# Splitting the last output tile, and two changes to a hand-written instruction plan, in a fused attention and feed-forward kernel

## The chip, the core and the metric

The kernel runs on one core of a Trainium2 chip. The metric is device time in microseconds for one execution, lower being better; the time quoted for a kernel is the median of several executions. The core has a matrix engine (TensorE, "PE" in the profile, with its weight loads listed as "PEld"), a vector engine (DVE), a scalar engine (ACT), a general engine (POOL) and a queue engine (SP) that here does nothing but issue transfers. Each engine runs its own instructions strictly in the order in which the program lists them, and waits on semaphores for the others.

## The reference

Two stages follow each other. The first is a block-wise linear attention with decay over 4 batches of 8 heads, 768 positions and 64 channels; the second a feed-forward layer on the 3072 tokens that result.

```python
for b in range(nb):                                   # blocks of 64 positions
    intra = einsum('bhic,bhjc->bhij', qb, kb) * Dmask
    intra = einsum('bhij,bhjd->bhid', intra, vb)
    inter = einsum('bhid,bhde->bhie', qb * lam_pow, kv_state)
    out[:, :, sl] = intra + inter
    kv_state = lam_block * kv_state + einsum('bhsd,bhse->bhde', kb * rev_pow, vb)
...
h = x @ w_in                                          # [3072, 512] @ [512, 2048]
g = where(h >= 1, h, where(h <= -1, 0, (h + 1) ** 2 / 4))
return g @ w_out                                      # [3072, 2048] @ [2048, 512]
```

## The kernel before

**Tiles.** The kernel works on 24 chunks of 128 positions (six to a batch) and on 6 stages of 512 tokens (four chunks each). For each chunk c it loads k and v (`ld`, 256 KB each) and for each pair of chunks q (`lq`, 512 KB), multiplies q and k by powers of lambda while casting to bfloat16 (`cast`, `cq`), transposes both, computes masked scores and the chunk's output, and updates a running state with keys and values. A stage then multiplies its 512 tokens by `w_in` (16 steps `l1`), applies the activation (ACT `r`, then three DVE steps `g`), and multiplies by `w_out` (16 steps `l2`: four tiles of 128 tokens, each in four steps `kg` of four matmuls). Each finished tile of 128 x 512 results is copied from PSUM to SBUF by ACT (`y`, line 398) and stored by SP (`st`, line 402).

**Names and lines.** The steps that the text follows are: `t` (transpose of keys; on PE for chunks 0 to 5, line 263, and as a transfer on the SP queue from chunk 6 on, line 284, tile kT); `qT` (transpose of queries; as transfers on SP from pair 3 on, line 287); `kb` and `kT` (copies of transposed keys from PSUM by DVE, lines 273 and 280); `u` (state update on PE, line 293) and `ub` (its cast by ACT, line 297); `s` (scores on PE, line 304 for chunks 0 to 3 and 312 after) and `m` (mask, DVE, lines 320 and 322); `o` (chunk output on PE, lines 329 and 332) and `x` (its copy by ACT into the tokens of the stage, line 339); `la` (the first four `l1` steps of stage 0 on three of its four chunks, line 353); `l1` (line 360); `l2` (line 393). Loads of k and v stand on line 439 (x1f and x2f in the profile), of q on line 435 (x0f), the casts of k on line 240 and of q on line 244 (tiles ks and qs), those of v on line 258 (vi).

**The order of the work** is written by a planner in the kernel itself, `run_plan`. Each step is entered with `add(key, engine, ns, function, needs, due, ...)`: an assumed duration, the steps that it needs, and for some a due time. The planner walks through an assumed time, gives each engine as its next step the ready one with the earliest due time, and in the end emits all instructions in that order. The times only decide the order: on the chip each engine follows the order and waits for what is really late. A step that becomes ready earlier in the plan is placed earlier in its engine's list.

A transfer's arrival is assumed from a single stream with a rate per step (`dma`). For loads of k and v from chunk 8 on, and of q from pair 4 on, 5000 ns are added:

```python
if x.key[0] in ("ld", "lq") and x.key[1] >= (FAR if x.key[0] == "ld" else FAR // 2):
    x.end += SLACK
```

On SP a transposing transfer has due -2 and a load a due time of 0 or a little more, so that a transpose that is ready goes ahead of a load; a load becomes ready when the buffer of the chunk six earlier (k, v) or the pair three earlier (q) has been cast. Before SP may issue a transfer, the plan asks that the third one back has been moved (`RING = 3`). A transpose counts as ready 2000 ns after its cast on POOL (`XSL`). Due times of the steps `l1` and `l2` lie 1057 ns apart from 22000 on in the order of `l_seq`, where they alternate between one stage's `l2` and the next one's `l1`; those of the steps of a chunk are counted back from the first `l1` that needs it (`o_due`), for scores another 2500.

**PSUM.** There are eight banks: two for `ph`, two for `py`, one each for `pt`, `pu`, `ps` and `po`. Outputs of `l2` use `py`, those of `l1` `ph`. The transposes `t` of chunks 0 to 5 use `pt`, which is also the second score bank of chunk 3 and of the chunks after it.

Of the kernel before, what the change touches and what calls it, by code (L numbers as in the profile page):

```python
# [23 lines left out]
def kernel(  # L24
# [31 lines left out]
    LD = 6  # L56
    LQ, NQ2 = 3, 3
    NO = 8
    XQ = 3
    RW, NR = 2, 3  # L60
    XT, NQT, NQK, RING = 6, 4, 4, 3
# [99 lines left out]

    LAT, FILL = 70, 170
    FAR, SLACK, XSL = 8, 5000, 2000
    ops, OPS = [], {}

    class Op:
# [9 lines left out]
    def run_plan(free):  # L176

        users = {x.key: [] for x in ops}
        for x in ops:
            x.needs = [OPS[y] for y in x.keys if y in OPS]  # L180
            for y in x.needs:
                users[y.key].append(x)
        left = {x.key: len(x.needs) for x in ops}
        topo = [x for x in ops if not x.needs]
        for x in topo:
            for u in users[x.key]:
                left[u.key] -= 1
                if left[u.key] == 0:
                    topo.append(u)
        assert len(topo) == len(ops)  # L190
        for x in reversed(topo):
            d = [u.due - u.ns - x.extra - LAT for u in users[x.key] if not u.dma]
            x.due = min(d + ([x.own] if x.own is not None else []), default=1e9)
            if x.dma or x.key[0] in ("l1", "l2"):
                x.due = x.own
        left = {x.key: len(x.needs) for x in ops}
        ready = {e: [] for e in free}
        for x in topo:
            if not x.needs:
                ready[x.eng].append((0, x))  # L200
        out_seq, xfer, dma_free = [], [0] * RING, 0
        while len(out_seq) < len(ops):
            t, e = min((max(free[e], min(r for r, _ in lst), xfer[-RING] if e == "SP" else 0), e)
                       for e, lst in ready.items() if lst)
            r, x = min(((r, x) for r, x in ready[e] if r <= t), key=lambda p: (p[1].due, p[0]))
            ready[e].remove((r, x))
            ns = x.ns + (720 if x.perf and free["POOL"] > t else 0)
            free[e] = t + ns
            x.t, x.end = t, t + ns + x.extra
            if x.dma:  # L210
                dma_free = max(dma_free, t + (1300 if e == "SP" else 2100)) + x.dma
                x.end = dma_free + 1400
                if x.key[0] in ("ld", "lq") and x.key[1] >= (FAR if x.key[0] == "ld" else FAR // 2):
                    x.end += SLACK
                if e == "SP":
                    xfer.append(dma_free)
            out_seq.append((t, len(out_seq), x))
            for u in users[x.key]:
                left[u.key] -= 1
                if left[u.key] == 0:  # L220
                    ready[u.eng].append((max(y.t if y.eng == u.eng and y.key != u.gate else y.end + (XSL if u.eng == "SP" and y.eng == "POOL" and u.dma == 640 else LAT) for y in u.needs), u))
        for t, _, x in sorted(out_seq, key=lambda p: p[:2]):
            if DBG:
                print(f"{t / 1e3:9.3f} {x.due / 1e3:9.3f} {x.eng:5s} {x.ns:6.0f} {x.key}")
            x.fn()
# [161 lines left out]
                op=AX.mult)  # L387

    def f_l2(s, ms, kg):
        if kg == 0:  # L390
            py_t[s, ms] = pp_y.tile([128, d_model], F32, name="py", tag="py")
        for ko in range(4 * kg, 4 * kg + 4):
            nc.tensor.matmul(py_t[s, ms], lhsT=gT[s][:, ko, ms * 128:(ms + 1) * 128], rhs=w_out_sb[:, ko, :],  # L393
                             start=(ko == 0), stop=(ko == FO - 1))

    def f_y(s, ms):
        osb[s, ms] = op.tile([128, d_model], F32, name="osb", tag="osb")
        nc.scalar.copy(out=osb[s, ms], in_=py_t[s, ms])  # L398

    def f_st(s, ms):  # L400
        m0 = s * MS + ms * 128
# [78 lines left out]
    for c in range(NCH):  # L480
        od, cb = o_due(c), c % NCB
        lastu = c - 1 if cb else c - 2
        m = c // 2
        e = "DVE" if c < CPS else "POOL"
        add(("cast", c, 1), e, 690 if e == "DVE" else 1060, lambda c=c, eng=(nc.vector if e == "DVE" else nc.gpsimd): cast(c, eng),
            [("ld", c, 1), ("cast", c - 1, 1), ("t", c - NQK), ("u", c - NQK)])
        add(("cast", c, 2), "ACT", 640, lambda c=c: cast_v(c),
            [("ld", c, 2), ("o", c - NV), ("u", c - NV), ("cast", c - 1, 2)])
        for i in range(2 if c % 2 == 0 else 0):
            old = ("tq", m - NQK // 2, i)  # L490
            add(("cq", m, i), "POOL", 1060, lambda m=m, i=i: cast_q(m, i, nc.gpsimd),
                [("lq", m), ("cq", m, 0) if i else None, old, ("qT",) + old[1:]])
            if m < XQ:
                add(("tq", m, i), "PE", mm(*[128] * 4), lambda m=m, i=i: f_tq(m, i),
                    [("cq", m, i)] + ([("kT", c - 1), ("m", c - 1, 1), ("tq", m, 0) if i else None] if c >= CPS else []),
                    due=od - 6000, extra=FILL)
                add(("qT", m, i), "ACT", 600, lambda m=m, i=i: f_qT(m, i), [("tq", m, i)])
            else:
                add(("qT", m, i), "SP", 1200, lambda m=m, i=i: f_qx(m, i), [("cq", m, i), ("o", 2 * (m - NQ2) + 1)], due=-2, dma=640)
        if c < XT:  # L500
            add(("t", c), "PE", mm(*[128] * 4), lambda c=c: f_t(c),
                [("cast", c, 1), ("kT", c - 1), ("kb", c - 1, 0), ("kb", c - 1, 1), ("m", c - 1, 1) if c > 2 else None,
                 ("qT", m, 0) if c >= CPS and c % 2 == 0 and m < XQ else None, ("qT", m, 1) if c >= CPS and c % 2 == 0 and m < XQ else None],
                due=od - 6000, extra=FILL)
        else:
            add(("t", c), "SP", 1200, lambda c=c: f_kx(c), [("cast", c, 1), ("m", c - NQT, 1)], due=-2, dma=640)
        if CPS <= c < XT:
            add(("kT", c), "DVE", 450, lambda c=c: f_kT(c), [("t", c), ("m", c - NQT, 1)])
        for hi in range(2 if c < CPS else 0):
            add(("kb", c, hi), "DVE", 365, lambda c=c, hi=hi: f_kb(c, hi), [("t", c), ("s", c - NKB, 1)])  # L510
        if cb < NCB - 1:
            add(("u", c), "PE", mm(*[128] * 4), lambda c=c: f_u(c),
                [("cast", c, 1), ("cast", c, 2), ("ub", lastu, 0), ("ub", lastu, 1), ("u", lastu)], due=od - 4000, extra=FILL)
            for hi in range(2):
                add(("ub", c, hi), "ACT", 372, lambda c=c, hi=hi: f_ub(c, hi), [("u", c), ("o", c - NUB + 1)])
        if c >= CPS:
            add(("s", c, 0), "PE", mm(*[128] * 4) + 190, lambda c=c: f_s2(c),
                [("kT", c) if c < XT else ("t", c), ("qT", m, 0), ("qT", m, 1), ("m", c - 1, 0), ("m", c - 1, 1)], due=od - 2500, extra=FILL)
        for h in range(2):
            if c < CPS:  # L520
                add(("s", c, h), "PE", mm(*[128] * 4), lambda c=c, h=h: f_s(c, h),
                    [("kb", c, 0), ("kb", c, 1), ("qT", m, 0), ("qT", m, 1), ("m", c - 1, 0) if not h else ("t", c)], due=od - 3000 + 100 * h, extra=FILL)
            add(("m", c, h), "DVE", 690, lambda c=c, h=h: f_m(c, h), [("s", c, h if c < CPS else 0), ("o", c - 3), ("m", c, 0) if h else None])
        add(("o", c), "PE", mm(*[128] * (12 if cb else 8)), lambda c=c: f_o(c),
            [("m", c, 1), ("cast", c, 2), ("ub", c - 1, 0) if cb else None, ("ub", c - 1, 1) if cb else None,
             ("x", c - 1), ("o", c - 1)], due=od, extra=FILL)
        add(("x", c), "ACT", 600, lambda c=c: f_x(c), [("o", c), ("x", c - 1), ("l1", (c // CPS - 2) * FO - 1)])
# [27 lines left out]
    for n2, (_, s, ms, kg) in enumerate(l2_order):  # L555
# [3 lines left out]
        else:  # L559
            need = [("g", (s * FO + 4 * kg + 3) // RW)]  # L560
        y = s * CPS + ms
        add(("l2", n2), "PE", mm(*[512] * 4), lambda a=(s, ms, kg): f_l2(*a),
            need + [("w", 1, kg), ("l2", n2 - 1), ("y", y - 2) if kg == 0 else None], due=l_due[2, s, ms, kg], extra=FILL)
        if kg == 3:
            add(("y", y), "ACT", 600, lambda a=(s, ms): f_y(*a), [("l2", n2), ("y", y - 1), ("st", y - NO)])
            add(("st", y), "SP", 550, lambda a=(s, ms): f_st(*a), [("y", y), ("st", y - 1)], due=0.055, dma=780)

# [31 lines left out]
```

## Time and profile before

| what | value |
|---|---|
| time, median of 4 runs | 226.08 us (225.9, 226.05, 226.1, 229.04) |
| time of the profiled execution | 227.34 us |
| its span, first to last instruction | 225.5 us |
| PE, busy | 206.8 us, 92% |
| DVE, busy | 141.0 us, 63% |
| ACT, busy | 123.9 us, 55% |
| POOL, busy | 62.3 us, 28% |
| moved by transfers | 34.40 MB, 153 GB/s over the span |
| granted clock of PE, mean | 0.996 |

The page gives for each engine the busy time, its share of the span and the number of instructions. The row of digits for an engine cuts the span into 40 equal slices and gives the busy share of each in tenths. Times in the views count from the first instruction. In the timeline a line reads: start, duration, engine, line of the code, operation, what is written and read, the number of instructions merged, and in brackets the idle time ahead of it with what ended it. The duration of a merged line runs from the first start to the last end. "SPq" is the time that the SP queue took to issue a transfer, not the transfer itself; the DMA view gives the time from the start of the issue to the landing.

### The profile page before, as it was taken

How to read it: one execution, taken by the hardware profiler on the slowest of the kernel's cores; microseconds unless marked ns; L12 is line 12 of the kernel's file. 1: busy time of each engine (PE TensorE's matmuls, PEld its weight loads, DVE VectorE, ACT ScalarE, POOL GpSimd, SP SyncE). 2: the span in 40 equal slices, each digit the busy share in tenths (PEclk: the TensorE clock that was granted, in tenths of full speed). 3: DMA queues.
4: the chain of work that ended last, by engine and by line, in shares of the span. 5: the costliest groups of instructions: out<-in, count | busy, mean ns of one | idle time of the engine just before them, and what ended most of it. 6: DMA issues, size and time to landing. Idle time of an engine off the chain costs nothing.

```text
span 225.5 us, 4659 instructions
## 1 busy us (share of the span) xinstructions
PE 206.8 (92%) x1888; PEld 135.4 (60%) x1888; DVE 141.0 (63%) x216; ACT 123.9 (55%) x222; POOL 62.3 (28%) x65
## 2 busy tenths in 40 slices
PE   0597996999997989999999999999999999999992
PEld 0486533677576777777766766777767644444440
DVE  4577395889958855697555668577565564464200
ACT  3556767547448466557637556676645544554121
POOL 7380084217616150746131027430000000000000
PEclk9999999999999999999999999999999999999998
DMA  5999999999797899999999799979201101111121
GB/s 134 242 189 201 196 239 186 179 214 221 123 257 124 215 160 204 133 245 134 241 149 324 217 260 229 208 168 158 41 33 49 47 0 49 47 47 46 47 96 48
DMA packets 89830, 34.40 MB, mean 153 GB/s; under 512 B 70352, under 2 KB 86736, under 8 KB 89808
## 3 DMA queue, kind: packets, MB, share of 16 engines
q1 hardware_dynamic: 85440, 29.89, 64.1%
q0 software_dynamic: 4224, 4.19, 11.6%
q8 instruction: 15, 0.25, 0.5%
q14 instruction: 7, 0.06, 0.1%
q10 hardware_dynamic: 144, 0.00, 0.0%
HBM read 27.27 MB, written 6.29 MB: 149 GB/s over the span
## 4 chain that ended last, share of the span: by engine, by line
PE 73%; DMA 17%; SPq 4%; POOL 2%; ACT 1%; issue 1%; POOLq 0%
PE py L393 35%; PE ph L360 29%; DMA x1f<-in_k_dram 5%; DMA w_in_sb<-in_moe_w_in_dram 4%; DMA x2f<-in_v_dram 4%; PE po L332 3%; PE ps L312 3%; SPq L439 3%; DMA x0f<-in_q_dram 2%; DMA kT<-ks 2%; PE po L329 1%; POOL qs L244 1%; PE pu L293 1%; SPq L435 1%; POOL w_in_sb L154 1%
## 5 line engine op out<-in xcount | busy, mean ns | idle before, releaser
L368 ACT ACTIVATE r<-ph,one 128x512 bf16<-128x512 f32 (+2 forms) x96 | 64.8, 679 | 56.9 <-PE ph L360 39.1
L393 PE MATMUL py<-w_out_sb,gT 128*128 128x512 bf16 x384 | 95.4, 379 | 0.0
L360 PE MATMUL ph<-xT,w_in_sb 128*128 128x128 bf16 (+2 forms) x880 | 94.0, 255 | 0.2 <-ACT r L368 0.2
L360 PEld LDWEIGHTS <-w_in_sb 128*128 128x128 bf16 x880 | 65.3, 98 | 23.5 <-issue 1.0
L393 PEld LDWEIGHTS <-gT 128*128 128x128 bf16 x384 | 35.5, 98 | 33.5 <-DVE gT L384 0.2
L376 DVE TENSOR_SCALAR t<-r 128x1024 bf16<-128x1024 bf16 x48 | 26.5, 551 | 40.8 <-ACT r L368 40.8
L379 DVE TENSOR_TENSOR w<-r,t 128x1024 bf16<-128x1024 bf16 x48 | 38.9, 810 | 1.5
L384 DVE TENSOR_TENSOR gT<-w,t 128x1024 bf16<-128x1024 bf16 x48 | 38.5, 801 | 1.6
L240 POOL TENSOR_TENSOR ks<-x1f,tab_k 128x512 bf16<-128x512 f32 x20 | 25.2, 1260 | 46.9 <-DMA x1f<-in_k_dram 19.5
L244 POOL TENSOR_TENSOR qs<-x0f,tab_q 128x512 bf16<-128x512 f32 x24 | 27.1, 1149 | 29.8 <-DMA x0f<-in_q_dram 20.6
L398 ACT COPY osb<-py 128x512 f32<-128x512 f32 x24 | 14.1, 586 | 16.3 <-PE py L393 12.8
L322 DVE TENSOR_TENSOR sc<-ps,causal 128x512 bf16<-128x512 f32 x20 | 13.8, 688 | 13.8 <-PE pt L312 13.8
L339 ACT CAST xT<-po 128x512 bf16<-128x512 f32 x24 | 14.1, 588 | 8.9 <-PE po L332 5.9
L332 PE MATMUL po<-sc,vi 128*128 128x128 bf16 x192 | 18.9, 224 | 0.0
L258 ACT CAST vi<-x2f 128x512 bf16<-128x512 f32 x24 | 14.8, 618 | 5.9 <-DMA x2f<-in_v_dram 5.8
L297 ACT CAST ubd<-pu 64x256 bf16<-64x256 f32 x40 | 14.6, 365 | 5.1 <-PE pu L293 4.7
L332 PEld LDWEIGHTS <-vi 128*128 128x128 bf16 x192 | 14.9, 101 | 2.3 <-issue 0.4
L329 PE MATMUL po<-qT,ubd 128*128 128x128 bf16 x80 | 14.7, 221 | 0.2 <-ACT xT L339 0.2
L322 DVE TENSOR_TENSOR sc<-pt,causal 128x512 bf16<-128x512 f32 x20 | 13.6, 680 | 0.0
L293 PE MATMUL pu<-vi,ks 128*128 128x128 bf16 x80 | 8.2, 228 | 2.2 <-ACT vi L258 2.1
L312 PE MATMUL ps<-qT,kT 64*128 64x128 bf16 x80 | 7.9, 219 | 2.1 <-DMA kT<-ks 2.1
L263 PE MATMUL pt<-ident,ks 128*128 128x128 bf16 x24 | 2.8, 248 | 7.2 <-DVE ks L240 7.0
(50 smaller groups left out, 81.0 us busy)
## 6 DMA issues: line engine op xcount, KB each, us to landing
x1f<-in_k_dram SPq DMA_DIRECT2D x24, 256.0 KB, 4.9
x0f<-in_q_dram SPq DMA_DIRECT2D x12, 512.0 KB, 5.7
x2f<-in_v_dram SPq DMA_DIRECT2D x24, 256.0 KB, 4.8
out_dram<-osb SPq DMA_DIRECT2D x24, 256.0 KB, 2.4
w_in_sb<-in_moe_w_in_dram POOLq DMA_DIRECT2D x4, 512.0 KB, 9.0
w_out_sb<-in_moe_w_out_dram POOLq DMA_DIRECT2D x4, 512.0 KB, 8.7
qT<-qs SPq DMA_TRANSPOSE x18, 4.0
kT<-ks SPq DMA_TRANSPOSE x18, 3.6
```

Of the source, the lines that this page charges most:

```text
L240: eng.tensor_tensor(ks[c], qkv_ld[c, 1], _bc(tab_k[:, c % NCB, :], 2, D), op=AX.mult)
L244: eng.tensor_tensor(qs[m, e], qkv_ld[m, 0][:, :, e], _bc(tab_q[:, e, m % (NCB // 2), :], 2, D), op=AX.mult)
L258: nc.scalar.copy(out=v_out(vi[c % NV]), in_=qkv_ld[c, 2].rearrange("p (a b) d -> p a b d", b=2))
L322: nc.vector.tensor_tensor(sc_sb[c][:, g], pst[c, g], _bc(causal, 1, HP), op=AX.mult)
L329: nc.tensor.matmul(po[:, hp], lhsT=ubd[(c - 1) % NUB][:, hp, :], rhs=q_cols(c, hp), start=True, stop=False)
L332: nc.tensor.matmul(po[:, hp], lhsT=vi[c % NV][:, hp, hi].rearrange("p a d -> p (a d)"), rhs=sc_sb[c][:, hi, hp, :], start=(cb == 0 and hi ...
L360: nc.tensor.matmul(ph[:, j * m:(j + 1) * m], lhsT=w_in_sb[:, ko, (ni + j) * 128:(ni + j + 1) * 128], rhs=xT[s][:, ko, part * m:(part + 1) ...
L368: nc.scalar.activation(out=r_t[grp][:, i, cs], in_=ph_t[s, ni, part][:, cs], func=AF.Relu, bias=one[:, 0:1])
L376: nc.vector.tensor_scalar(t_t[grp], r, 0.5, 1.0, op0=AX.mult, op1=AX.min)
L379: nc.vector.tensor_tensor(w_t[grp], r, t_t[grp], op=AX.subtract)
L384: nc.vector.tensor_tensor(gT[s][:, f - RW * n:f, part * m:(part + 1) * m], w_t[grp].rearrange("p a (b m) -> p (a b) m", m=m), t_t[grp].rea ...
L393: nc.tensor.matmul(py_t[s, ms], lhsT=gT[s][:, ko, ms * 128:(ms + 1) * 128], rhs=w_out_sb[:, ko, :], start=(ko == 0), stop=(ko == FO - 1))
```

## The change

The change has three parts. The last output tile, of stage 5 and tokens 384 to 511 of it, is computed in two column parts of 384 and 128 columns: the first runs through all 16 blocks of the inner dimension in a bank of `py`, then the second in a bank of `ph`. Each part is copied by DVE, where ACT copied the tile, and stored by a transfer of its own. Second, the 5000 ns that the planner adds to arrivals become 2500 for k and v of chunks 8 and 9 and q of pair 4. Third, the transpose `t` of chunk 3 no longer needs the mask `m` of chunk 2 (the condition begins at chunk 4).

```diff
+    LAST, CUT = (NST - 1, CPS - 1), 384
...
+    NEAR = 2500
...
                 if x.key[0] in ("ld", "lq") and x.key[1] >= (FAR if x.key[0] == "ld" else FAR // 2):
-                    x.end += SLACK
+                    x.end += SLACK if (x.key[1] if x.key[0] == "ld" else 2 * x.key[1]) >= 10 else NEAR
...
     def f_l2(s, ms, kg):
+        if (s, ms) == LAST:
+            i = kg // 2
+            if kg % 2 == 0:
+                pl, nm = ((pp_y, "py"), (pp_h, "ph"))[i]
+                py_t[s, ms, i] = pl.tile([128, d_model], F32, name=nm, tag=nm)
+            cs = (slice(0, CUT), slice(CUT, d_model))[i]
+            for ko in range(FO // 2 * (kg % 2), FO // 2 * (kg % 2 + 1)):
+                nc.tensor.matmul(py_t[s, ms, i][:, cs], lhsT=gT[s][:, ko, ms * 128:(ms + 1) * 128],
+                                 rhs=w_out_sb[:, ko, cs], start=(ko == 0), stop=(ko == FO - 1))
+            return
...
+    def f_y2(i):
+        s, ms = LAST
+        cs = (slice(0, CUT), slice(CUT, d_model))[i]
+        if i == 0:
+            osb[s, ms] = op.tile([128, d_model], F32, name="osb", tag="osb")
+        (nc.vector.tensor_copy, nc.vector.tensor_copy)[i](osb[s, ms][:, cs], py_t[s, ms, i][:, cs])
+
+    def f_st2(i):
+        s, ms = LAST
+        m0 = s * MS + ms * 128
+        cs = (slice(0, CUT), slice(CUT, d_model))[i]
+        nc.sync.dma_start(out=out[m0:m0 + 128, cs], in_=osb[s, ms][:, cs])
...
-                [("cast", c, 1), ("kT", c - 1), ("kb", c - 1, 0), ("kb", c - 1, 1), ("m", c - 1, 1) if c > 2 else None,
+                [("cast", c, 1), ("kT", c - 1), ("kb", c - 1, 0), ("kb", c - 1, 1), ("m", c - 1, 1) if c > 3 else None,
...
-        add(("l2", n2), "PE", mm(*[512] * 4), lambda a=(s, ms, kg): f_l2(*a),
+        add(("l2", n2), "PE", mm(*[512] * 4) if (s, ms) != LAST else mm(*[CUT if kg < 2 else d_model - CUT] * 8), lambda a=(s, ms, kg): f_l2(*a),
...
-        if kg == 3:
+        if (s, ms) == LAST:
+            if kg % 2:
+                i = kg // 2
+                add(("y2", i), "DVE", (460, 200)[i], lambda i=i: f_y2(i), [("l2", n2), ("y", y - 1)])
+                add(("st2", i), "SP", 550, lambda i=i: f_st2(i), [("y2", i), ("st", y - 1)], due=1, dma=(600, 250)[i])
+        elif kg == 3:
```

## The prediction

> **What bounds the kernel now.** I read the page first, then the waits of TensorE, then the SP queue and POOL around the longest waits, then the last microseconds.
>
> ```profile
> span 225.5 us, 4659 instructions
> PE 206.8 (92%) x1888; PEld 135.4 (60%) x1888; DVE 141.0 (63%) x216; ACT 123.9 (55%) x222; POOL 62.3 (28%) x65
> DMA  5999999999797899999999799979201101111121
> ```
>
> TensorE (PE) is busy 92% of the span, and the DMA row is at nine tenths for the first 60% of it. So time can come only from the start, the end, and PE's few waits. The waits view of PE alone gives these (total, times, longest):
>
> ```profile
> PE pt L263 <- DVE ks L240: 7.0, 1, 7.0
> PE ps L312 <- DMA kT<-ks: 2.1, 2, 1.6
> PE pu L293 <- ACT vi L258: 2.1, 2, 1.4
> PE ps L304 <- DVE kbd L273: 0.7, 3, 0.3
> ```
>
> The 7.0 us is the first load and the change doesn't touch it. The timeline of PE places three others; the bracket is the idle time ahead of the line and what ended it:
>
> ```profile
> 35.53 0.38 PE L293 MATMUL pu<-vi,ks 128*128 128x128 bf16 x4 [1.45 <-ACT vi L258]
> 73.39 0.23 PE L312 MATMUL ps<-qT,kT 64*128 64x128 bf16 x1 [1.58 <-DMA kT<-ks]
> 81.52 0.23 PE L312 MATMUL ps<-qT,kT 64*128 64x128 bf16 x1 [0.57 <-DMA kT<-ks]
> ```
>
> The score groups on transposed keys from the queue begin with chunk 6 (59.85, then 63.33), so the waits of 1.58 and 0.57 are the scores of chunks 8 and 9: PE stands until their transposed keys land. The data were there long before. POOL cast chunk 8's keys at 59.82 (first line), but the SP queue began their transpose only at 70.87:
>
> ```profile
> 59.82 1.22 POOL L240 TENSOR_TENSOR ks<-x1f,tab_k 128x512 bf16<-128x512 f32 x1
> 61.89 1.17 SPq L435 DMA_DIRECT2D x0f<-in_q_dram  x1
> 63.11 1.13 SPq L439 DMA_DIRECT2D x1f<-in_k_dram  x1
> 64.34 1.25 SPq L439 DMA_DIRECT2D x2f<-in_v_dram  x1
> 65.69 5.01 SPq L287 DMA_TRANSPOSE qT<-qs  x2
> 70.87 1.19 SPq L284 DMA_TRANSPOSE kT<-ks  x1
> ```
>
> The queue's order is the planner's, and the planner believed that the loads of chunk 8 arrive 5 us late. The end, from the timeline:
>
> ```profile
> 217.67 0.59 ACT L398 COPY osb<-py 128x512 f32<-128x512 f32 x1 [2.87 <-PE py L393]
> 221.13 0.59 ACT L398 COPY osb<-py 128x512 f32<-128x512 f32 x1 [2.87 <-PE py L393]
> 221.74 0.33 SPq L402 DMA_DIRECT2D out_dram<-osb  x1
> ```
>
> After PE's last matmul come one copy (0.59), one store (2.0 to landing, by the DMA view of that window) and 1.8 to the span's end.
>
> **Part 1, the last tile.** PE does 16 matmuls of 384 columns and 16 of 128 in place of 16 of 512. Spacings from the trace: 512 columns 3.45/16 = 0.216 (the copies at 217.67 and 221.13 stand 3.46 apart), 384 columns 0.65/4 = 0.163 (the L353 group, 22.14 to 22.79), 128 columns 0.89/16 = 0.056 (the L360 groups of the second stage, each matmul with its own weight load). 16 x 0.163 + 16 x 0.056 = 3.50, so PE ends 0.05 later. The 16 more weight loads are in the 0.056. The first part's copy and store issue (DVE, then SP) run while PE does the 0.89 of the second part; were that cover gone they would cost their 0.55 + 0.33. The copy that counts is now 128 columns on DVE, which is idle after 209.9. No row has it: below it stands the 12-column cast, 0.19, above it the 512-column copy of bf16 from PSUM, 0.42. A line from 12 columns (0.19) to 512 columns of f32 from PSUM (0.68, L322) gives 0.30 at 128, which I take: 0.29 less than 0.59.
>
> The second store moves 64 KB, not 256. Upper bound: it lands after 2.0 like a whole store. Lower: 192 KB at the pace at which two loads of 256 KB landed one after the other (63.11 + 6.8 = 69.9, 64.34 + 6.3 = 70.6, so 0.7 to 0.8 each) is 0.6 less, 1.4. The first part's 192 KB is issued some 0.6 earlier in the same queue and may hold it up, so I take 1.6: 0.4 less. Part 1: 0.05 - 0.29 - 0.4 = **-0.65** (-0.1 with the slow copy and no shorter landing, -0.95).
>
> The Trainium skill ("DMA: Bandwidth & Descriptors", "Rules for kernel authors") speaks against this part: it wants small transfers joined, since one under 64 KB is mostly overhead. Its fit ("Anatomy of one DMA", a fixed 2.0 us and bytes over 436 GB/s) was made for another queue; the measured 2.0 for 256 KB already lies below its 2.6. By its slope alone the landing would give 0.45 in place of my 0.4, an estimate, and part 1 would be -0.7.
>
> False waits between the two parts I leave out: stage by stage PE reads slices of gT while DVE writes others of the same tile without a wait, and the two parts have a bank each.
>
> **Part 2, chunks 8 and 9.** The planner's arrival of loads (8, *), (9, *) and lq 4 falls by 2.5. In the plan the q and k casts of chunk 8 then end 2.5 earlier, and transposes go ahead of loads (due -2 against due above 0). Following run_plan's queue rule by hand: qT 4 (two) and kT 8 take the SP places just behind lq 5, in front of k and v of chunk 10; kT 9 goes in front of lq 6 and k of chunk 12. Nothing is issued that wasn't before.
>
> PE's order moves with it. Scores 8 (due 68293, against 70622 for the L393 step then in line) become ready in the plan 2.4 earlier and take the place after chunk 8's state update (68.77 to 69.00 in the trace), ahead of one L393 step and two L360 steps: 0.86 + 2 x 0.89 = 2.65 that ran from 69.00 to 71.8. So PE will want kT 8 at 69.0, not 71.8.
>
> When does kT 8 land? The transposes now start at 63.11, behind k 9 (60.59 + 4.0 = 64.6), v 9 (61.21 + 4.5 = 65.7) and lq 5 (61.89 + 7.1 = 69.0). Before, qT 4 took 3.70 of its pair's 5.01 to issue and got in at 69.39, when lq 5 had landed; kT 8 landed 1.3 after its issue ended. Early case: from 65.7 to 70.6 lq 5 and chunk 10's loads landed, 1 MB in 4.9, so the 512 KB of lq 5 alone may take 2.4 and land at 68.1; kT 8 is let in at 68.5, as qT 4 was 0.4 behind lq 5, and lands at 69.8. Late case: lq 5 at 69.0 and three transposes behind it at 0.95 each (71.4 to 73.35 is two of them): 71.9. I take 70.4, nearer the early end because two transposes can be let in while lq 5 runs. Wait at scores 8: 70.4 - 69.0 = 1.4 against 1.58, **-0.2** (0.8 to 2.9, so -0.8 to +1.3). The order moves, the wait stays.
>
> kT 9 landed at 81.5, behind lq 6 and k 12, which now stand after it. From v 11 (72.78 + 4.5 = 77.3) to k 12 (75.35 + 5.5 = 80.9) those two took 3.5, so it lands near 78. PE wants it after v's and L360's steps of then; its place moves up by one to two steps (0.9 to 1.8) from 80.95 - 0.2, so 79 to 80. Wait **-0.57** (0 to -0.57). Next late is chunk 10: its k and v loads go out some 6 us later, behind three transposes. Its keys landed at 82.02 + 4.0 = 86.0, its scores ran at 89.0; with two loads more ahead of kT 10 (1.6) it has 1.4 to spare before and about 0.6 after PE's gain. Cost nothing, 1 us if that cover is gone.
>
> **Part 3, kT of chunk 3.** The transpose t 3 loses its wait for the second mask of chunk 2 and goes before state update 3 on PE. It feeds the copy on DVE, which ran without a gap behind that same mask (19.22), so nothing comes sooner. The plan also puts the output of chunk 3 ahead of the first L353 step, which costs PE up to 0.65 of filling around 21. That runs into the wait of 1.45 at 35.53, which is for v of chunk 4 (its load, issued at 26.93, landed after 7.9) and doesn't move. **0** (-0.2 to +0.3); without that wait it would be +0.65.
>
> **Sum.** -0.65 - 0.2 - 0.57 + 0 = -1.4. The profiled execution took 227.34 (span 225.5 and 1.84 around it), so 225.9 for one like it; the median shown, 226.08, is 1.26 below it, so **224.7**. All bounds at their good ends: -0.95 - 0.8 - 0.57 - 0.2 = -2.5; at their bad ends with chunk 10 late: -0.1 + 1.3 + 0 + 0.3 + 1 = +2.5.
>
> **Rivals.** (a) The wait at scores 8 goes too: kT 8 lands by 69.0, or PE's order has steps left to run. For it: the casts are done by 61.04, and the two loads of chunk 10, 512 KB, no longer stand in front. Against: lq 5 still does. It gives -0.65 - 1.58 - 0.57 = -2.8: 223.3. (b) Slower: PE asks at 69.0, and the transposes stay held behind lq 5 and land as before at 73.35. PE is in order, so the L393 and L360 steps behind scores 8 stand with it: the wait is 4.35, +2.77, and with -0.65 and -0.57 the sum is +1.55: 227.6. It decides from 71.8 on (69.0 + 1.58 + 0.65 + 0.57), and is over 1% slower from 74.1. For it: 3.70 for one transpose's issue shows how hard a q load blocks; against: only k 9, v 9 and lq 5 are ahead, not lq 5 and chunk 10. (c) The plan's shift changes nothing on PE and only the end pays: 225.4. Against: both waits are on transposes that it moves.
>
> **How the numbers follow.** The forecast has 0.42, (a) 0.36, (b) 0.14, (c) 0.08. A measurement of this kernel tells about 1% (2.3 us) from no change. Faster by over 1%, below 223.8: nearly all of (a) and a little of the forecast, 0.40. Slower: the part of (b) where chunk 10 is late as well, 0.10. Within: 0.50. The range goes from just under (a), 222.9, to 226.8, which leaves out the upper part of (b); the forecast's own is 223.8 to 225.6.
>
> **What would show it.** Right: two L393 groups of 384 and 128 columns at the end, a DVE copy of some 0.3, a landing under 2.0; qT and kT ahead of the loads of chunk 10; a wait of about 1.4 in front of the score group near 69; none at the next; the wait near 35.5 still there. Wrong: a wait near 69 that is gone or above 2.9, a new one at chunk 10, or an SP order other than the one told.

## The result and the profile after

The changed kernel took 225.69 us (median), the kernel before, on the same chip, 226.6: a ratio of 0.996, 95% interval 0.9945 to 0.9974. That is 0.9 us less (0.6 to 1.2), inside the range and some two thirds of the 1.4 us forecast. The experiments show that the parts do not share it as the prediction had it: the first gains what was forecast, the second measured under half of what it was given and is not clear of zero, and the third, costed at nothing, loses some 0.7 us.

The page of the changed kernel's profiled execution, which took 225.26 us:

```profile
span 223.6 us, 4691 instructions
PE 206.8 (93%) x1904; PEld 136.3 (61%) x1904; DVE 148.9 (67%) x218; ACT 123.5 (55%) x221; POOL 64.2 (29%) x65
DMA  5999999999599999989999999989211001110212
```

TensorE (PE) is busy as long as before, 206.8, with 16 more matmuls; the span is 1.9 shorter. PE's waits (total, times, longest), the five that matter:

```profile
PE pt L265 <- DVE ks L242: 7.8, 2, 7.7
PE ph L362 <- ACT r L370: 1.1, 3, 0.5
PE pt L272 <- ACT qT L278: 0.7, 1, 0.7
PE po L334 <- DVE sc L322: 0.5, 1, 0.5
PE ps L314 <- DMA kT<-ks: 0.4, 1, 0.4
```

Transposed keys from the queue now cost PE 0.4, not 2.1, and the wait for chunk 4's v (1.4) is off the list. Three waits are new or longer: 1.1 for ScalarE's activation r (0.2 before), 0.7 for its copy of qT, and 0.5 for a mask of DVE ahead of the output steps near 21. The first load, which the change does not touch, took 0.7 longer here, but the scores of chunk 3 begin at 19.68 in both profiles. PE's timeline places the waits (idle time ahead of a line and what ended it in the bracket):

```profile
34.78 0.38 PE L272 MATMUL pt<-ident,qs 128*128 128x128 bf16 x4 [0.67 <-ACT qT L278]
35.30 0.38 PE L295 MATMUL pu<-vi,ks 128*128 128x128 bf16 x4
...
69.19 0.23 PE L314 MATMUL ps<-qT,kT 64*128 64x128 bf16 x1 [0.38 <-DMA kT<-ks]
...
78.47 0.23 PE L314 MATMUL ps<-qT,kT 64*128 64x128 bf16 x1
```

The scores of chunk 8 run at 69.19, not 73.39; those of chunk 9 at 78.47 without a wait. The SP queue shows why:

```profile
61.14 1.14 SPq L460 DMA_DIRECT2D x0f<-in_q_dram  x1
62.38 3.81 SPq L289 DMA_TRANSPOSE qT<-qs  x2
66.36 1.20 SPq L286 DMA_TRANSPOSE kT<-ks  x1
67.61 0.58 SPq L464 DMA_DIRECT2D x1f<-in_k_dram  x1
68.29 0.53 SPq L464 DMA_DIRECT2D x2f<-in_v_dram  x1
68.86 1.16 SPq L464 DMA_DIRECT2D x1f<-in_k_dram  x1
70.12 1.14 SPq L464 DMA_DIRECT2D x2f<-in_v_dram  x1
71.43 2.63 SPq L286 DMA_TRANSPOSE kT<-ks  x1
```

Transposes stand ahead of chunk 10's loads, which go out at 67.61 and 68.29. The end, from the timeline of all engines, and the two stores in the DMA view of the last microseconds (KB each, median us from issue to landing):

```profile
218.92 1.06 PE L399 MATMUL ph<-w_out_sb,gT 128*128 128x128 bf16 x16
219.12 0.56 DVE L417 COPY osb<-py 128x384 f32<-128x384 f32 x1 [10.36 <-PE py L399]
219.71 0.96 SPq L423 DMA_DIRECT2D out_dram<-osb  x2
220.02 0.29 DVE L417 COPY osb<-ph 128x128 f32<-128x128 f32 x1 [0.34 <-PE ph L399]
```

```profile
out_dram<-osb SPq DMA_DIRECT2D x1, 192.0 KB, 1.9
out_dram<-osb SPq DMA_DIRECT2D x1, 64.0 KB, 1.6
```

The 384 columns are copied (0.56) and their store issued while PE still does the 128 columns; then come a copy of 0.29 and a landing of 1.6. From PE's last matmul to the end of the span it is 3.6 (219.98 to 223.56), before 4.4 (221.09 to 225.51).

### The profile page after: what moved, and what is told of

Same layout as the page of the kernel before. It is cut to its first block, busy times and chain, and to the rows that moved or that the text cites. A ratio compares the mean times of both kernels' runs of the same rounds, so it can differ in the third digit from the quotient of the medians.

```text
span 223.6 us, 4691 instructions
## 1 busy us (share of the span) xinstructions
PE 206.8 (93%) x1904; PEld 136.3 (61%) x1904; DVE 148.9 (67%) x218; ACT 123.5 (55%) x221; POOL 64.2 (29%) x65
## 4 chain that ended last, share of the span: by engine, by line
PE 78%; DMA 10%; ACT 3%; SPq 3%; DVE 2%; issue 2%; POOL 1%; ACTq 0%; POOLq 0%
PE ph L362 32%; PE py L405 31%; DMA x2f<-in_v_dram 4%; DMA x0f<-in_q_dram 4%; PE po L334 4%; PE ps L314 3%; PE pu L295 2%; PE po L331 2%; SPq L464 1%; ACT r L370 1%; DMA kT<-ks 1%; PE py L399 1%; DVE sc L322 1%; PE py L355 1%; PE ph L355 1%
## 5 line engine op out<-in xcount | busy, mean ns | idle before, releaser
L405 PE MATMUL py<-w_out_sb,gT 128*128 128x512 bf16 x368 | 92.1, 379 | 0.0
L378 DVE TENSOR_SCALAR t<-r 128x1024 bf16<-128x1024 bf16 x48 | 27.9, 582 | 39.4 <-ACT r L370 39.4
L405 PEld LDWEIGHTS <-gT 128*128 128x128 bf16 x368 | 33.9, 98 | 31.4 <-DVE gT L386 0.2
L386 DVE TENSOR_TENSOR gT<-w,t 128x1024 bf16<-128x1024 bf16 x48 | 42.1, 876 | 1.7
L246 POOL TENSOR_TENSOR qs<-x0f,tab_q 128x512 bf16<-128x512 f32 x24 | 29.1, 1234 | 35.9 <-DMA x0f<-in_q_dram 30.7
L381 DVE TENSOR_TENSOR w<-r,t 128x1024 bf16<-128x1024 bf16 x48 | 38.3, 798 | 1.3
L410 ACT COPY osb<-py 128x512 f32<-128x512 f32 x23 | 13.5, 587 | 12.0 <-PE py L405 10.1
L331 PEld LDWEIGHTS <-ubd 128*128 128x128 bf16 x80 | 7.9, 99 | 1.6
```

Of the source, the lines that this page charges most:

```text
L246: eng.tensor_tensor(qs[m, e], qkv_ld[m, 0][:, :, e], _bc(tab_q[:, e, m % (NCB // 2), :], 2, D), op=AX.mult)
L331: nc.tensor.matmul(po[:, hp], lhsT=ubd[(c - 1) % NUB][:, hp, :], rhs=q_cols(c, hp), start=True, stop=False)
L378: nc.vector.tensor_scalar(t_t[grp], r, 0.5, 1.0, op0=AX.mult, op1=AX.min)
L381: nc.vector.tensor_tensor(w_t[grp], r, t_t[grp], op=AX.subtract)
L386: nc.vector.tensor_tensor(gT[s][:, f - RW * n:f, part * m:(part + 1) * m], w_t[grp].rearrange("p a (b m) -> p (a b) m", m=m), t_t[grp].rea ...
```

## The experiments

Profiles of the same kernel lie up to 2 us apart, so verdicts rest on ratios with their 95% intervals (the kernels of one series, measured beside the kernel before on one chip), and the profiles say only where PE waits. There are four series: the parts and the whole; then three more that take part 3 and part 2 apart.

**Each part alone, and the whole.** Part 1 alone takes the branch for the last tile and nothing else:

```diff
+    LAST, CUT = (NST - 1, CPS - 1), 384
...
+        if (s, ms) == LAST:
+            i = kg // 2
...
+            return
```

> Only the last tile in two parts; the plan as before. Between the trace of before and that of the whole change the stretch from PE's last matmul to the span's end fell from 4.4 to 3.7. The prediction's term says -0.65 (-0.1 to -0.95): about 0.997 of before. Theory A (the three terms add, and the end is about a third to a half of the gain): 0.6 to 0.8 us less, PE's waits as before (1.45 or so at v of chunk 4, some 1.6 and 0.6 at the scores of chunks 8 and 9). Theory B (what the plan's part gains is given back later, so that the end is nearly the whole measured gain of 0.9): the same kernel, and no more than 0.1 short of the whole change's ratio in this call.

Measured: 0.9963 (0.9937 to 0.9989), 0.84 us less. Its end is the one just shown:

```profile
220.80 0.96 SPq L423 DMA_DIRECT2D out_dram<-osb  x2
221.11 0.29 DVE L417 COPY osb<-ph 128x128 f32<-128x128 f32 x1 [0.34 <-PE ph L399]
```

In all eleven profiles with the split end, 3.6 us follow PE's end; with the old end it is 4.4. Part 1 is worth what its row says, within its interval.

Part 2 alone:

```diff
+    NEAR = 2500
...
-                    x.end += SLACK
+                    x.end += SLACK if (x.key[1] if x.key[0] == "ld" else 2 * x.key[1]) >= 10 else NEAR
```

> Only the 2500 in place of 5000 for chunks 8 and 9 and q of pair 4. The queue's order of the whole change, the end as before. Theory A: waits at the scores of chunks 8 and 9 fall from 2.1 together to 0.4 or less, up to 0.9 of it comes back where ACT waits for v loads around 110 and 131 and PE for ACT's activation: 0.8 to 1.0 us less. Theory B: it comes back entirely, 0.3 us or less gained.

Measured: 0.9985 (0.9964 to 1.0006), 0.34 us less and not clear of zero. In its profile PE waits 1.04 at the scores of chunk 8 and not at those of chunk 9. But a wait is there that the profile of before does not have (this execution was the slowest of its twelve, 227.59 us against a median of 225.22, so its size is not to be relied on; the changed kernel's profile has the same wait, smaller):

```profile
113.84 1.03 PE L361 MATMUL ph<-xT,w_in_sb 128*128 128x256 bf16 x8 [1.50 <-ACT r L369]
```

Part 3 alone:

```diff
-  ("m", c - 1, 1) if c > 2 else None,
+  ("m", c - 1, 1) if c > 3 else None,
```

> Only the transpose of chunk 3 freed from the mask of chunk 2. Both theories of the record: nothing, -0.2 to +0.3 us; the first 512-column l1 step starts some 0.6 later (26.5 against 25.85 in the two traces) and the wait for v of chunk 4 near 35 takes that up, shrinking by as much. Rival: it is this part that moves v casts ahead in ACT's order, and the PE waits for the activation near 112 and 132 are then seen here.

Measured: 1.0042 (1.0014 to 1.0069), 0.95 us **more**. This is the term that the prediction had at zero. And the whole change beside the three:

> The whole change again, beside its parts on one chip. Theory A: its ratio is the product of the three parts' within 0.002, near 0.994 to 0.996. Theory B: it is that of the last tile alone.

Measured: 1.0011 (0.998 to 1.0042); the product of the parts is 0.9990.

**Without part 3, and what part 2 gives back.** If part 3 costs and parts 1 and 2 gain, the change without part 3 must be the best version. Its edit is those of parts 1 and 2:

> The change without its third part. The third part alone measured 1.0042, the first 0.9963, the second 0.9985. Theory C (the third part costs 0.5 to 0.9 us, since it takes from PE the filling around 21 and the wait for v of chunk 4 that should cover this is only 0.7 in the traces of the first two parts, not 1.45): 0.9948 of before, 1.1 to 1.2 us less, and 0.5 to 0.9 us under the whole change in this call. Rival (the third part's slowdown was chance, and the whole change gains the 0.996 first shown): equal to the whole change within 0.3 us.

Measured: 0.9946 (0.992 to 0.9972), 1.2 us less than before. The whole change beside it:

> The whole change beside the kernels above on one chip. Theory C: 0.5 to 0.9 us above the one without the third part, 0.996 to 1.001 of before. Rival: equal to it.

Measured: 0.9985 (0.996 to 1.001).

The wait for r in part 2's profile came with a wait of ScalarE itself. First the changed kernel's ScalarE timeline, then PE's:

```profile
110.79 0.62 ACT L260 CAST vi<-x2f 128x512 bf16<-128x512 f32 x1 [1.95 <-DMA x2f<-in_v_dram]
...
131.50 0.62 ACT L260 CAST vi<-x2f 128x512 bf16<-128x512 f32 x1 [2.83 <-DMA x2f<-in_v_dram]
```

```profile
112.05 1.03 PE L362 MATMUL ph<-xT,w_in_sb 128*128 128x256 bf16 x8 [0.34 <-ACT r L370]
132.76 1.03 PE L362 MATMUL ph<-xT,w_in_sb 128*128 128x256 bf16 x8 [0.53 <-ACT r L370]
```

ScalarE is in order: while its cast of a later v stands 1.95 and 2.83 for the load, the activations behind it stand too, and PE runs out of r. In the version without part 3 the same casts stood shorter, and PE did not wait there:

```profile
109.47 0.62 ACT L260 CAST vi<-x2f 128x512 bf16<-128x512 f32 x1 [0.71 <-DMA x2f<-in_v_dram]
...
128.53 0.62 ACT L260 CAST vi<-x2f 128x512 bf16<-128x512 f32 x1 [0.44 <-DMA x2f<-in_v_dram]
```

A later profile of this same version has the first of the two casts standing 2.77, and a wait of PE for r of 1.2:

```profile
111.07 0.62 ACT L260 CAST vi<-x2f 128x512 bf16<-128x512 f32 x1 [2.77 <-DMA x2f<-in_v_dram]
```

So it differs from one execution to the next: of the eleven profiles with part 2 five have such a wait after 100 us, of the seven without it none. From the profiles, means in us, seven without part 2 against ten with it (part 2 alone left out, as its execution was an outlier): chunk 6's state update to chunk 11's scores 42.66 and 41.87, from there to PE's end 123.96 and 124.42. By these means part 2 gains 0.8 and loses 0.5 later, of which the waits for r make 0.4. To take the loss away, the planned arrival of v from chunk 12 on was put 2.5 later, so that ScalarE's casts are planned later:

```diff
+                    if x.key[0] == "ld" and x.key[2] == 2 and x.key[1] >= 12:
+                        x.end += 2500
```

> As the kernel before it in this list, with 2500 more added to the planned arrival of v for chunks 12 to 23, which moves seven casts of v back in ACT's order and nothing on PE's or SP's. Theory D (the second part's gain is given back where ACT stands at casts of v planned 2 to 5 us earlier than in the kernel before, and PE at its activation behind them, 0 to 1.8 us from one execution to the next): no PE wait for the activation near 112 and 132, 0.3 to 0.8 us less than without the 2500. Rival (those waits are seldom in an execution without a profile): the same within 0.2 us, or slower if state updates now come late.

Measured: 0.997 (0.9935 to 1.0004), no better than without it (0.9946 in the same series), where theory D wanted 0.3 to 0.8 us less. Its one profile has no late wait for r, but the one without the edit in the same series had none either; waits of 0.4 to 0.5 for kT stand near 145 and 148 (another profile without this edit has one of 0.3 near 146). The remedy fails. That the waits behind the casts are where part 2's gain goes is read from the profiles and not shown: the one run meant to take them away did not get the gain back.

**What in part 3 costs.** Part 3 changes two orders on PE: the transposition of chunk 3 goes ahead of state update 3, and the output steps of chunk 3 go ahead of the first L353 step (some steps around chunk 5 follow). Theory C: the second costs. Part 3 with the old order of the second:

```diff
-             ("x", c - 1), ("o", c - 1)], due=od, extra=FILL)
+             ("x", c - 1), ("o", c - 1), ("la", 0) if c == 3 else None], due=od, extra=FILL)
```

> The third part alone, with one need more: the output of chunk 3 waits for the first of the early l1 steps, so that all orders are those of the kernel before but for the transpose of chunk 3 ahead of its state update. Theory C: within 0.1% of before, since the transpose itself gains nothing and the cost of the third part is the filling lost by the output going ahead. Rival (the transpose ahead of the state update is itself the cost): 1.003 to 1.005 as with the whole third part.

Measured: 1.0028 (1.0001 to 1.0054), between the two. Again, and on the whole change, with the two versions that it stands between:

> Part 3 alone with the output of chunk 3 held behind the first L353 step, a second time. Theory C: 1.000. Rival: 1.003 to 1.005. The first measurement, 1.0028 with an interval from 1.0001 to 1.0054, lay between.

Measured: 1.0009 (0.998 to 1.0037).

> All three parts, with one more need: the output of chunk 3 also waits in the plan for the first L353 step, so TensorE's order around 21 us is the old one and only the transposition ahead of state update 3 is left of part 3. Theory C (part 3 costs because the output steps ahead of the first L353 step): the whole loss goes, 0.9946 like parts 1 and 2 alone, about 224.3 us. Rival (the transposition itself costs, or anything that starts chunk 4's scores later): part 3's 0.3 to 0.5% stays, 0.998, about 225.0 us. From 0.996 to 0.997 it stays open.

Measured: 0.9965 (0.9933 to 0.9996).

> Parts 1 and 2 without part 3, a second time: 0.9946 as in the first measurement, and 0.3 to 0.5% below all three parts in the same call. If part 3 is worth nothing (the prediction's 0) the two agree within 0.1%.

Measured: 0.9955 (0.9918 to 0.9993).

> The change as it is, beside the three others on the same chip: by the product of its parts alone (0.9963, 0.9985 and 1.0042) 0.999; by its earlier measurements 0.996 to 1.001. Theory C wants it 0.3 to 0.5% above the version whose order is kept, the rival wants the two equal.

Measured: 0.996 (0.9932 to 0.9987): in this series part 3 cost 0.0005, within error. Then the other half without the first, by a need in the plan that makes the first L353 step wait for the output of chunk 3:

```diff
-  ("m", 2, 1))[i]], due=l_due[1, 0, 0, 0] - 1000, extra=FILL)
+  ("m", 2, 1))[i], ("o", 3)], due=l_due[1, 0, 0, 0] - 1000, extra=FILL)
```

> The kernel before with one more need in the plan: the first L353 step waits for the output of chunk 3, so TensorE takes them in part 3's order; the transposition of chunk 3 stays behind state update 3, and no part of the change is in it. Theory C (this order is part 3's cost): 1.003 to 1.005, some 226.3 us, with the wait of 0.5 ahead of the output steps near 21 and chunk 4's scores at 37.4 instead of 35.8. Rival (the transposition, or the orders around chunk 5 that follow from both edits, cost): 1.000 to 1.001.

Measured: 1.0012 (0.9988 to 1.0036). Its PE timeline:

```profile
21.16 0.27 PE L332 MATMUL po<-sc,vi 128*128 128x128 bf16 x2 [0.50 <-DVE sc L320]
...
32.75 0.39 PE L270 MATMUL pt<-ident,qs 128*128 128x128 bf16 x4
32.98 1.03 PE L360 MATMUL ph<-xT,w_in_sb 128*128 128x512 bf16 x4
33.84 0.39 PE L270 MATMUL pt<-ident,qs 128*128 128x128 bf16 x4
34.77 0.40 PE L293 MATMUL pu<-vi,ks 128*128 128x128 bf16 x4 [0.54 <-POOL ks L240]
```

The wait of 0.50 ahead of the output steps comes as expected, and 0.54 is left of the wait at state update 4; but chunk 4's scores ran at 36.45, not at the 37.4 that theory C wanted.

> Part 3 alone, beside the former on the same chip: 1.0042 as in the first measurement if its cost is real, 1.000 if the prediction's zero holds and the first measurement was a draw. Theory C wants it equal to the former, the rival 0.3 to 0.4% above it.

Measured: 1.0019 (0.9987 to 1.0052).

> Parts 1 and 2, and the output of chunk 3 ahead of the first L353 step without the transposition moved. Theory C: 0.3 to 0.5% above parts 1 and 2 alone, 0.998. Rival: equal to them, 0.995.

Measured: 0.9968 (0.994 to 0.9997), 0.26% above the next.

> Parts 1 and 2 alone on the same chip: 0.995, as measured twice (0.9946 and 0.9955).

Measured: 0.9942 (0.9917 to 0.9967).

Taken together, each measurement weighted by its interval: parts 1 and 2 give 0.9946 (0.9946, 0.9955, 0.9942), part 3 alone 1.0032 with an error of some 0.002 (1.0042, 1.0019). The whole change, 0.9971 over its four measurements, stands 1.0025 above parts 1 and 2, with the same error. So part 3 costs some 0.7 us (0.0032 x 226), and both ways of measuring it leave zero outside their error. The series scatter more than their intervals say, though: the whole change's 1.0011 and the main measurement's 0.996 have intervals that do not meet, and beside parts 1 and 2 it stood 1.0039 above them in one series and 1.0005 in another. The order of output steps alone gives 1.0012, and on parts 1 and 2 0.9968/0.9942 = 1.0026; the transposition alone gives 1.0028 and 1.0009, and on parts 1 and 2 0.9965/0.9955 = 1.0010. Each half seems to bear some 0.15%, and neither is told from zero by itself. Theory C as stated, the whole cost in one order, is not confirmed; how the cost splits stays open.

Where it shows on PE, from the profiles of part 3 alone and of parts 1 and 2, in PE's timeline:

```profile
33.84 0.39 PE L270 MATMUL pt<-ident,qs 128*128 128x128 bf16 x4
34.90 0.38 PE L270 MATMUL pt<-ident,qs 128*128 128x128 bf16 x4 [0.67 <-ACT qT L276]
```

```profile
31.79 0.39 PE L272 MATMUL pt<-ident,qs 128*128 128x128 bf16 x4
32.01 1.03 PE L362 MATMUL ph<-xT,w_in_sb 128*128 128x512 bf16 x4
33.17 0.40 PE L272 MATMUL pt<-ident,qs 128*128 128x128 bf16 x4
34.35 0.40 PE L295 MATMUL pu<-vi,ks 128*128 128x128 bf16 x4 [0.78 <-POOL ks L242]
35.79 0.23 PE L314 MATMUL ps<-qT,kT 64*128 64x128 bf16 x1
```

With parts 1 and 2, a step of four 512-column matmuls stands between the two transpositions of q and covers ScalarE's copy of the first; with part 3 the two stand side by side and PE waits 0.67. In exchange the wait at state update 4, 0.78 here, is gone. So part 3 trades a wait of 0.7 to 0.8 for 0.50 near 21, 0.67 and 0.15, and chunk 4's scores run at 37.5 instead of 35.8 (37.56 in the profile of before, which has the wait of 1.45). Most of that delay is taken up by the next wait, for chunk 6's loads. Chunk 6's state update, counted from the score group near 20 (L304 of before): 33.5 to 33.7 in all six profiles with part 3, none with a wait there; 32.4 to 34.1, mean 33.4, in seven without it, all but two with a wait of 0.55 to 1.17. Part 3 makes PE itself the limit there, so early loads no longer bring anything. That accounts for 0.2 of the 0.7 us; where the rest falls the profiles, with their scatter, do not show.

The two transpositions of q stand side by side only when both halves are in. In all five profiles of a half alone a step stands between them, as in the lines with the output steps ahead (32.75 to 33.84), and PE does not wait ahead of the second. The stretch up to chunk 6's state update, less the wait there, says the same: 33.5 to 33.7 with part 3, 32.2 to 32.9 with the old order (33.9 in the profile of before), 32.2 to 32.5 with the transposition alone, and 32.0 with the output steps alone, which has one L393 step (0.86) fewer in it and so 32.9 for equal work. So by the profiles part of the cost belongs to neither half alone; the times are too coarse to confirm it.

## Why the prediction was right or wrong

**Part 1 was right, step by step.** The 128-column copy took 0.29 (said 0.30), the second store landed in 1.6 (said 1.6), the first part's copy and issue were covered by PE's last matmuls. The sum was -0.65; the profiles show -0.8 between PE's end and the span's, and the measurement -0.84 (-0.25 to -1.4). Some 0.1 of the 0.8 lies behind the last landing (1.8 before, 1.6 to 1.7 after), a stretch that the sum left as it was. The Trainium skill's advice to join small stores ("DMA: Bandwidth & Descriptors", "Rules for kernel authors") did not hold for this last store: 64 KB landed 0.4 sooner than 256 KB, because the 192 KB ahead of it moved under PE's work. By the slope of its fit ("Anatomy of one DMA"), made for another queue, the estimate was 0.45, near the 0.4 measured.

**Part 2: the mechanism was right, two sizes were off.** PE's order and the SP order moved as worked out: PE asked for the keys of chunk 8 at 68.81 (69.19 - 0.38; said 69.0), and the wait at chunk 9 went. The first size is kT 8's landing, put at 70.4 with 69.8 as the early end: it was there at 69.2. Of the two bounds the q load's was the better one, and still too late: the load landed at 67.6 (61.14 + 6.5; said 68.1 to 69.0), and the second of the two q transposes was issued by 66.2, before it had. Eleven profiles give waits of 0 to 1.04 at this place, mean 0.6, where 1.4 was forecast. The second size is the base: the 2.15 at chunks 8 and 9 was that of one execution, and over seven profiles with the old order the two waits together come to 0.7 to 2.15, mean 1.4. So 0.8 was to be had, near the 0.77 said, by two errors that cancel: that is luck. **What fails is "cost nothing" for what goes late next.** The prediction looked at chunk 10, and chunk 10 did not wait. Some 0.5 went back after chunk 11's scores, by the profiles most of it where PE waits behind ScalarE's casts of later v near 111 and 131, in some executions; that this is the cause is not shown. With part 2 -0.34 is left (-0.8 to +0.1) of the 0.77.

**Part 3 was the step that was wrong.** It was put at 0 (-0.2 to +0.3) and measured +0.7. Its zero rested on a wait of 1.45 at state update 4 that "doesn't move" and takes up the 0.65. Three things were wrong. The 1.45 was a draw of that execution: the same wait is 0.7 to 0.8 in most profiles with the old order (1.05 in one), and in those six it ends with POOL's cast of chunk 4's keys, not with v. The price was worked out from too little: besides the order near 21, the two transpositions of q came to stand side by side (0.67 for ScalarE's copy), which the prediction's own sentence, +0.65 without that wait, does not contain. And the sign that was named for it, a wait near 35.5 still there, failed: the wait at state update 4 is gone, and one of 0.67 at the transposition ahead of it stands in its place. That the 0.65 is near the 0.7 measured is luck; the mechanism is more than the one step it was worked out from, and how the 0.7 splits stays open.

**The total.** -0.65 - 0.77 + 0 = -1.4 was forecast; the parts measured -0.84, -0.34 and +0.7, together -0.5, and the whole -0.9 in the main measurement, -0.7 if all four (0.996, 1.0011, 0.9985, 0.996) are weighted by their intervals. Parts and whole agree within their errors. Rival (a), which takes the whole wait at chunk 8 away, came near on its place: 0.38 was left in the profile. It fails on the total: part 2 measured 0.34 where it had 2.15, and part 3 cost. Rival (b) did not happen: kT 8 landed 4.2 earlier, not at 73.35. Rival (c), only the end pays, gives 225.4, and 226.08 x 0.996 is 225.2: nearest in time, and wrong in its reason, since part 2 moved both waits and part 3 cost what part 2 gained or more.

**The version that beats both** is parts 1 and 2 without part 3: 0.9946 over three measurements, 1.2 us less than before, against 0.7 to 0.9 for the change as it is. It is not told from part 1 alone (0.9963, 0.9937 to 0.9989).

## What to carry to other kernels

Work that is costed at nothing because a wait hides it needs that wait in more than one execution: a wait for a load is one draw, and the part of it that is always there is the cover. When a planner's orders are edited, read the whole new order on each engine: an output step and a transposition of keys, moved together, put two transpositions side by side 13 us later, which neither move did alone. A wait that is removed in front of in-order engines can return at the next late load, and that may be on another engine than the one watched.

## What the runs showed of the hardware

A last store of 64 KB lands in 1.6 us, one of 192 KB in 1.9 and one of 256 KB in 2.0: most of it does not depend on size, and what splitting saves is 0.4 of landing and 0.3 of the copy (0.59 on ScalarE for 512 columns, 0.29 on VectorE for 128). Behind a 512 KB load in the same queue, transposes took 3.81 to issue for a pair, and were let in before that load had landed (66.2 against 67.6). Waits for loads on one core differ by over 1 us between executions with the same order of these transfers in the queue (0.7 to 2.15 for the two waits on transposed keys in seven profiles), at a granted clock between 0.995 and 1.0.
